# Two-bank PSUM tiles for the AV of batch 0: one normalisation and one x evacuation for two blocks

## The chip, the cores and the metric

The kernel runs on one core of a Trainium2 chip. The metric is the device time of one execution in microseconds (us). Several executions are made of each kernel; one more view, the profile, records every instruction of one of them. Engines: PE is TensorE, DVE is VectorE, ACT is ScalarE, POOL is GpSimd, SP is SyncE, which here only issues loads and stores.

## The reference

Eight batches of attention against pooled keys and values, and a two-layer MLP over all tokens.

```python
# q, k, v: (8, 8, 576, 64); w_in: (512, 2048); w_out: (2048, 512)
k_p = k.reshape(B, H, 72, 8, D).mean(axis=3)          # pool 8 keys to one
v_p = v.reshape(B, H, 72, 8, D).mean(axis=3)
scores = np.matmul(q, k_p.transpose(0, 1, 3, 2)) / np.sqrt(D)
attn = softmax(scores)
x = np.matmul(attn, v_p)                              # (B, H, S, D) -> (B*S, 512)
h = x @ w_in
out = (h - np.tanh(h)) @ w_out                        # (4608, 512) float32
```

## The kernel before

The kernel does the attention of batch 0 first, then the MLP of 512 tokens at a time, with the attention of the next batch woven between the MLP's matmuls. "AV" is the product of the exponentials with the pooled values. A column of ones beside V gives the sum of the exponentials, so a normalisation is a reciprocal of 4 columns and a multiplication. A "turn" is a transpose done on PE; the "q tail" is the load of the q rows of a batch's last 64 tokens; `warm_pe` runs idle matmuls, whose results nobody reads, where PE would wait.

```python
def av_half(b, blk, half, x_sb, alloc):               # one block of 128 tokens, 4 heads
    ps = alloc([128, 4, D1], FP32, "x_ps")            # one PSUM bank
    for n in range(3):
        ... # three matmuls into ps
    rden = work.tile([128, 4, 1], FP32, name="rden", tag="rden", bufs=4)
    nc.vector.reciprocal(out=rden[:, :, :], in_=ps[:, :, D:D1])
    nc.vector.tensor_tensor(out=x_sb[:, half, :, :], in0=ps[:, :, 0:D],
        in1=rden[:, :, :].to_broadcast([128, 4, D]), op=ALU.mult)

def x_pe_transpose(b, blk, x_sb, fbs=(0, 4)):         # turn x on PE, copy it to xT on ACT
    ps = ps_any([128, f1 - f0, 128], FP32, "xT_ps")
    ...
    nc.scalar.copy(out=xT[:, f0:f1, pos : pos + 128 - p0], in_=ps[:, :, p0:128])
...
after(load_k(1), w1_dmas[1])                          # batch 1's keys: after a weight load
load_q(1, False)
load_main(v_pairs, v_raw[1], 1, 0, NM)
...
load_left(v_pairs, v_raw[1], 1, nc.scalar)            # loads that ACT issues, ahead of
load_q_tail(1, q_raws[1], nc.scalar)                  # its x copies
...
av_half(0, 2, 0, xs[2], ps_all)                       # AV, turns, and the first
x_pe_transpose(0, 0, xs[0], (0, 2))                   # halves of five MLP tiles,
...                                                   # woven by hand
mlp_h_mms(0, 4, 0, 2, (ps_o, "o_ps"))
nc.scalar.copy(out=q_bf[:QT, R, :, :], in_=t0[:QT, :, R, :])
for i in range(5):
    mlp_h_mms(0, i, 2, 4)                             # their second halves
    mlp_h_act(i, gts)
...
pool_k(1, nc.gpsimd, mid=(2, 3))                      # batch 1's keys, pooled on POOL;
...                                                   # two w2 loads issued in the middle
for u in range(16):                                   # MLP output of the first 512 tokens
    mlp_o(0, tb, qd * 4, qd * 4 + 4, gts, o_pools[tb])
    if u == 2:
        k_transpose(1, ps_any, (nc.vector.tensor_copy, nc.vector.tensor_copy))
    if u == 3:
        q_pe_transpose(1, (0, 1), "act")
    ...
```

The softmax here doesn't subtract the row's maximum and nothing guards it: scores larger than these inputs give would overflow.

## Time and profile before

| | |
|---|---|
| time, median of 3 | 300.64 us (300.51 to 300.65) |
| span in the profile | 299.1 us |
| PE busy | 97% |
| granted PE clock | 1.00 |
| AV stretch of batch 0 | 14.6 to 21.3 us |
| PE reaches the key transposes of batch 1 | 37.3 us |
| they start | 37.82 us |

This is the timeline of PE (start, length, engine, line, operation, output and inputs, and in brackets how long the engine was idle and for whom):

```profile
18.49 0.59 PE L428 MATMUL hT_ps<-xT,w1b 128*128 128x512 bf16 x2 [0.28 <-ACT xT L397]
...
37.82 0.45 PE L259 MATMUL kT_ps<-ident,kd 128*128 128x128 bf16 x5 [0.52 <-POOL kd L206]
```

The first is the end of the AV stretch: the first MLP matmul waits for ACT's copies of x. The second is the wait for the keys.

### The profile page before, as it was taken

To read this page: it belongs to the slowest core of one execution; us is meant where nothing else is said; L and a number is where in the kernel's file an instruction comes from. 1 tells how busy PE (TensorE), PEld (TensorE's weight loads), DVE (VectorE), ACT (ScalarE), POOL (GpSimd) and SP (SyncE) were. 2 spreads that over 40 slices of the span, in tenths; PEclk is the share of its full clock that TensorE was granted. 3 is DMA by queue.
4 is the path that set the end of the run, shared out by engine and by line. 5 is a ranking of instruction groups with operands and counts; after the bars stand their busy time and mean duration, and the time that the engine had idled before them with its cause. 6 is when DMAs were issued, how large, how long until landed. Compare 5 with 4: busy or idle time off the path is not lost.

```text
span 299.1 us, 4694 instructions
## 1 busy us (share of the span) xinstructions
PE 291.5 (97%) x1671; PEld 142.5 (48%) x1671; DVE 159.1 (53%) x343; ACT 149.4 (50%) x283; POOL 115.5 (39%) x110
## 2 busy tenths in 40 slices
PE   7989999999999999999999999999999999999994
PEld 3454455544544454445444554455445544444443
DVE  5658665673547444753476247716680758108600
ACT  4647583666146633654265516650665166126511
POOL 8500904871496109922971089307940000000000
PEclk9999999999999999999999999999999999999999
DMA  7999999849854998699648974897431430111032
GB/s 251 226 211 278 311 227 310 263 87 328 234 113 99 271 297 134 117 302 245 107 88 235 300 167 94 242 294 159 97 66 35 95 92 0 37 70 36 0 72 70
DMA packets 66183, 49.79 MB, mean 166 GB/s; under 512 B 39920, under 2 KB 52976, under 8 KB 66160
## 3 DMA queue, kind: packets, MB, share of 16 engines
q1 hardware_dynamic: 58832, 42.94, 56.0%
q0 software_dynamic: 4752, 4.72, 9.4%
q10 hardware_dynamic: 2576, 1.84, 2.3%
q8 instruction: 13, 0.21, 0.3%
q14 instruction: 10, 0.08, 0.1%
HBM read 36.70 MB, written 9.44 MB: 154 GB/s over the span
## 4 chain that ended last, share of the span: by engine, by line
PE 85%; DMA 9%; POOL 4%; issue 0%; SPq 0%; ACT 0%; DVE 0%; POOLq 0%
PE o_ps L456 40%; PE hT_ps L428 37%; DMA w1b<-in_moe_w_in_dram 4%; PE x_ps L346 4%; DMA k_raw<-in_k_dram 4%; PE s_ps L298 3%; POOL k_raw L198 1%; DMA out_dram<-o_sb 1%; POOL k_raw L203 1%; POOL kd L206 1%; POOL w2b L510 0%; PE xT_ps L390 0%; POOL v_raw L576 0%; PE qT_ps L171 0%; POOL w1b L503 0%
## 5 line engine op out<-in xcount | busy, mean ns | idle before, releaser
L456 PE MATMUL o_ps<-w2b,gT 128*128 128x512 bf16 x560 | 134.4, 380 | 0.0
L441 DVE TENSOR_TENSOR gT<-hT_ps,t_sb 128x512 bf16<-128x512 f32 x144 | 98.9, 691 | 57.7 <-ACT t_sb L439 57.6
L428 PE MATMUL hT_ps<-xT,w1b 128*128 128x512 bf16 x576 | 126.9, 379 | 0.3 <-ACT xT L397 0.3
L439 ACT ACTIVATE t_sb<-hT_ps 128x512 f32<-128x512 f32 x144 | 85.6, 597 | 38.3 <-PE hT_ps L428 37.5
L428 PEld LDWEIGHTS <-w1b 128*128 128x128 bf16 x576 | 55.9, 98 | 66.5 <-issue 0.4
L456 PEld LDWEIGHTS <-gT 128*128 128x128 bf16 x560 | 52.5, 98 | 52.0 <-issue 1.4
L465 ACT COPY o_sb<-o_ps 128x512 f32<-128x512 f32 x33 | 19.3, 585 | 75.2 <-PE o_ps L456 75.2
L359 DVE RECIPROCAL rden<-x_ps 128x4 f32<-128x4 f32 x80 | 14.2, 177 | 52.5 <-PE x_ps L346 52.0
L360 DVE TENSOR_TENSOR x_sb<-x_ps,rden 128x256 bf16<-128x256 f32 x80 | 34.0, 425 | 3.5 <-DMA xT<-x_sb 0.6
L148 POOL CAST q_bf<-q_raw 128x2048 bf16<-128x2048 f32 x6 | 11.3, 1888 | 59.9 <-issue 34.8
L198 POOL TENSOR_TENSOR k_raw<-k_raw 128x1280 f32<-128x1280 f32 x7 | 20.2, 2886 | 27.4 <-DMA k_raw<-in_k_dram 16.6
L317 ACT ACTIVATE E<-s_ps 128x288 bf16<-128x288 f32 x60 | 21.4, 410 | 13.2 <-PE s_ps L298 13.0
L346 PE MATMUL x_ps<-VB,E 128*128 128x130 bf16 x240 | 20.8, 221 | 0.4 <-ACT xT L397 0.3
L346 PEld LDWEIGHTS <-E 128*128 128x128 bf16 x240 | 16.9, 98 | 8.8 <-DVE VB L230 0.6
L216 POOL TENSOR_TENSOR v_raw<-v_raw 128x1280 f32<-128x1280 f32 x6 | 17.4, 2898 | 0.0
L298 PE MATMUL s_ps<-qT,KB 128*128 128x288 bf16 (+5 forms) x128 | 17.0, 290 | 0.2
L298 PEld LDWEIGHTS <-KB 128*128 128x128 bf16 (+1 forms) x128 | 7.0, 96 | 10.2 <-issue 3.5
L527 PE MATMUL warm_ps<-xT 128*128 128x512 bf16 x29 | 10.2, 465 | 1.3 <-DVE xT L539 1.3
L206 POOL TENSOR_TENSOR kd<-k_raw 128x640 bf16<-128x640 f32 x7 | 10.8, 1540 | 0.5
L203 POOL TENSOR_TENSOR k_raw<-k_raw 128x640 f32<-128x640 f32 x7 | 10.8, 1541 | 0.5
L397 ACT CAST xT<-xT_ps 128x256 bf16<-128x256 f32 (+1 forms) x14 | 5.8, 436 | 8.5 <-PE xT_ps L390 5.1
L219 POOL TENSOR_TENSOR v_raw<-v_raw 128x640 f32<-128x640 f32 x6 | 9.3, 1544 | 0.5
(73 smaller groups left out, 100.7 us busy)
## 6 DMA issues: line engine op xcount, KB each, us to landing
k_raw<-in_k_dram SPq DMA_DIRECT2D x7, 1024.0 KB, 5.9
q_raw<-in_q_dram SPq DMA_DIRECT2D x7, 1024.0 KB, 10.2
v_raw<-in_v_dram SPq DMA_DIRECT2D x7, 1024.0 KB, 9.3
out_dram<-o_sb SPq DMA_DIRECT2D x38, 128.0 KB, 2.4
out_dram<-o_sb SPq DMA_DIRECT2D x16, 256.0 KB, 3.7
w1b<-in_moe_w_in_dram POOLq DMA_DIRECT2D x4, 512.0 KB, 14.2
w2b<-in_moe_w_out_dram POOLq DMA_DIRECT2D x4, 512.0 KB, 16.9
k_raw<-in_k_dram SPq DMA_DIRECT2D x7, 128.0 KB, 5.8
```

The costliest lines, as they stand in the source:

```text
L198: first = eng.tensor_tensor(out=r[:, :, 0:4, :], in0=r[:, :, 0:4, :], in1=r[:, :, 4:8, :], op=ALU.add)
L216: eng.tensor_tensor(out=r[:, :, 0:4, :], in0=r[:, :, 0:4, :], in1=r[:, :, 4:8, :], op=ALU.add)
L298: nc.tensor.matmul(dst[p : p + w], lhsT=KB[b % 2][:, o : o + w], rhs=qTs[b][:, m, c0:c1], start=True, stop=True,)
L317: nc.scalar.activation(out=E[:, t, half * hs : (half + 1) * hs], in_=ps[:, :], func=ACT.Exp, scale=SCALE)
L346: nc.tensor.matmul(ps[:, 2 * n : 2 * n + 2, :].rearrange("p h d -> p (h d)") if n < 2 else ps.rearrange("p (a s) d -> p a s d", s=2)[:, :, ...
L359: nc.vector.reciprocal(out=rden[:, :, :], in_=ps[:, :, D:D1])
L360: nc.vector.tensor_tensor(out=x_sb[:, half, :, :], in0=ps[:, :, 0:D], in1=rden[:, :, :].to_broadcast([128, 4, D]), op=ALU.mult,)
L428: nc.tensor.matmul(h_tiles[i][:, :], lhsT=w1b[:, fb, i * 128 : (i + 1) * 128], rhs=xT[:, fb, tok0 : tok0 + TG], start=(fb == 0), stop=(fb ...
L439: nc.scalar.activation(out=t_sb[:, :], in_=h_ps[:, :], func=ACT.Tanh)
L441: nc.vector.tensor_sub(out=gT[:, :], in0=h_ps[:, :], in1=t_sb[:, :])
L456: nc.tensor.matmul(o_ps[:, :], lhsT=gts[i][:, tb * 128 : (tb + 1) * 128], rhs=w2b[:, i, :], start=(i == 0), stop=(i == NHID - 1),)
L465: (nc.vector.tensor_copy if g == 0 and tb % 2 else nc.scalar.copy)(out=o_sb[:, :], in_=o_ps[:, :])
```

## The change

The intent is to halve the number of DVE and ACT instructions in the AV stretch of batch 0, for which PE waits there (0.39 us for DVE, 0.29 and 0.28 for ACT in the profile before). In the same profile, twice the elements take less than twice the time: a DVE multiplication out of PSUM 425 ns for 128x256 and 691 ns for 128x512, an ACT copy of x 375 and 590 ns. PSUM becomes one tile of eight banks with banks assigned by hand. A pair of blocks takes two neighbouring banks, so that one reciprocal, one multiplication and one copy serve both. Order and queues of all loads stay. The order of PE's work changes too, and the sequence has one idle matmul more (6 instead of 5).

```diff
+    psum = ctx.enter_context(tc.tile_pool(name="psum", bufs=1, space=PSUM))
+    PS = psum.tile([128, 8, 512], FP32, name="PS")
...  (ps_h, ps_o and ps_a become rotations over banks 0-2, 3-4 and 5-7)
+    def av_pair(p, half, b0):
+        ps = PS[:, b0 : b0 + 2, 0 : 4 * D1].rearrange("p k (h d) -> p k h d", d=D1)
+        for k in range(2):
+            av_mms(0, 2 * p + k, half, ps[:, k, :, :])
+        rden = work.tile([128, 2, 4, 1], FP32, name="rden2", tag="rden2")
+        nc.vector.reciprocal(out=rden[:, :, :, :], in_=ps[:, :, :, D:D1])
+        nc.vector.tensor_tensor(out=x0[:, 2 * p : 2 * p + 2, half, :, :],
+            in0=ps[:, :, :, 0:D], in1=rden[:, :, :, :].to_broadcast([128, 2, 4, D]), op=ALU.mult)
+    def x0_turn(blks, half, b0, eng):
+        ...  # turns of one or two blocks into one bank
+        eng(out=xT[:, 2 * half : 2 * half + 2, c : c + n * 128], in_=ps.rearrange("p f i c -> p f (i c)"))
+    av_pair(0, 0, 2)
+    av_pair(1, 0, 5)
+    av_pair(0, 1, 0)
+    warm_pe(1)
+    x0_turn((0, 1), 0, 7, nc.scalar.copy)
+    av_pair(1, 1, 2)
+    warm_pe(1)
+    x0_turn((2, 3), 0, 5, nc.scalar.copy)
+    warm_pe(2)
+    h_open(3, 4)
+    x0_turn((0, 1), 1, 7, nc.scalar.copy)
...  (h_open(0), h_open(1), last turns, h_open(2), h_open(4); the av_half sequence of before goes)
```

More of the change, by code (lines that the diff above doesn't have):

```diff
@@ L57, with bank, __init__, tile @@
     opool = ctx.enter_context(tc.tile_pool(name="opool", bufs=4))
-    ps_h = ctx.enter_context(tc.tile_pool(name="ps_h", bufs=3, space=PSUM))
-    ps_o = ctx.enter_context(tc.tile_pool(name="ps_o", bufs=2, space=PSUM))
-    ps_a = ctx.enter_context(tc.tile_pool(name="ps_a", bufs=3, space=PSUM))
+    psum = ctx.enter_context(tc.tile_pool(name="psum", bufs=1, space=PSUM))
+    PS = psum.tile([128, 8, 512], FP32, name="PS")
+    def bank(i, shape):
+        n = 1
+        for d in shape[1:]:
+            n *= d
+        v = PS[:, i, 0:n]
+        if len(shape) == 3:
+            return v.rearrange("p (a b) -> p a b", a=shape[1])
+        if len(shape) == 4:
+            return v.rearrange("p (a b c) -> p a b c", a=shape[1], b=shape[2])
+        return v
+    class Banks:
+        def __init__(self, *ids):
+            self.ids, self.n = ids, 0
+        def tile(self, shape, dtype=None, name=None, tag=None):
+            self.n += 1
+            return bank(self.ids[(self.n - 1) % len(self.ids)], shape)
+    ps_h = Banks(0, 1, 2)
+    ps_o = Banks(3, 4)
+    ps_a = Banks(5, 6, 7)
     ctx.enter_context(tc.manual_schedule())
@@ L81 @@
     warm = const.tile([128, 1], FP32, name="warm")
+    x0 = const.tile([128, 4, 2, 4, D], BF16, name="x0")
     VB = [const.tile([128, 3 * NM, D1], BF16, name=f"VB{i}") for i in range(2)]
@@ L336, in scores_tail, with av_mms @@
         )
-    def av_half(b, blk, half, x_sb, alloc):
+    def av_mms(b, blk, half, ps):
         E = E_tiles[b]
@@ L341, in av_half @@
         c0 = blk * 128 if blk < 4 else S - 128
-        ps = alloc([128, 4, D1], FP32, "x_ps")
         for n in range(3):
@@ L357, in av_half @@
             )
+    def av_half(b, blk, half, x_sb, alloc):
+        ps = alloc([128, 4, D1], FP32, "x_ps")
+        av_mms(b, blk, half, ps)
         rden = work.tile([128, 4, 1], FP32, name="rden", tag="rden", bufs=4)
@@ L424, in mlp_h_mms @@
         if f0 == 0:
-            p, tag = pool or (ps_h, "hT_ps")
-            h_tiles[i] = p.tile([128, TG], FP32, name="hT_ps", tag=tag)
+            h_tiles[i] = ps_h.tile([128, TG]) if pool is None else pool
         for fb in range(f0, f1):
@@ L521, in after, with warm_pe @@
             )
-    warm_ps = ps_o.tile([128, 512], FP32, name="warm_ps", tag="o_ps")
-    def warm_pe(n, cols=512):
+    def warm_pe(n, cols=512, b0=4):
         for _ in range(n):
             nc.tensor.matmul(
-                warm_ps[:, 0:cols], lhsT=zeros[:, 0:128], rhs=zeros[:, 0:cols], start=True, stop=True
+                bank(b0, [128, cols]), lhsT=zeros[:, 0:128], rhs=zeros[:, 0:cols], start=True, stop=True
             )
@@ L613, in q_turn, with v_pe_pool @@
         )
-    def v_pe_pool(t0, t1, turn):
-        ps = ps_any([128, t1 - t0, 1, D], FP32, "v_ps")
+    def v_pe_pool(t0, t1, turn, b0=None):
+        shape = [128, t1 - t0, 1, D]
+        ps = ps_any(shape, FP32, "v_ps") if b0 is None else bank(b0, shape)
         for j in range(POOL):
@@ L628, in ps_b1 @@
         return ps_a.tile(shape, dtype, name=name, tag="ps_a")
-    ps_all = ps_any
     q_turn(nc.scalar.copy, 0, 2)
@@ L655 @@
     v_left(VB[0], v_ps[:, 0, :, :], nc.vector)
-    vs = v_pe_pool(0, NM, ident)
+    vs = v_pe_pool(0, NM, ident, 4)
     v_main(VB[0], vs, nc.vector, 0, 2)
@@ L660 @@
     load_q_tail(1, q_raws[1], nc.scalar)
-    xs = [new_x() for _ in range(4)]
     gts = []
-    ps_o2 = lambda sh, dt, name: ps_o.tile(sh, dt, name=name, tag="o_ps")
-    ps_h2 = lambda sh, dt, name: ps_h.tile(sh, dt, name=name, tag="hT_ps")
-    warm_pe(2)
-    av_half(0, 0, 0, xs[0], ps_all)
-    av_half(0, 1, 0, xs[1], ps_all)
-    av_half(0, 2, 0, xs[2], ps_all)
-    x_pe_transpose(0, 0, xs[0], (0, 2))
-    av_half(0, 3, 0, xs[3], ps_all)
-    warm_pe(1)
-    x_pe_transpose(0, 1, xs[1], (0, 2))
@@ L673 @@
-    ps_any = ps_b1
-    av_half(0, 0, 1, xs[0], ps_h2)
-    warm_pe(1)
-    x_pe_transpose(0, 2, xs[2], (0, 2))
-    av_half(0, 1, 1, xs[1], ps_b1)
-    warm_pe(1)
-    x_pe_transpose(0, 3, xs[3], (0, 2))
-    av_half(0, 2, 1, xs[2], ps_o2)
-    mlp_h_mms(0, 0, 0, 2)
-    x_pe_transpose(0, 0, xs[0], (2, 4))
-    av_half(0, 3, 1, xs[3], ps_b1)
-    mlp_h_mms(0, 1, 0, 2)
-    x_pe_transpose(0, 1, xs[1], (2, 4))
-    mlp_h_mms(0, 2, 0, 2)
-    x_pe_transpose(0, 2, xs[2], (2, 4))
-    x_pe_transpose(0, 3, xs[3], (2, 4))
@@ L689 @@
-    mlp_h_mms(0, 3, 0, 2, (ps_o, "o_ps"))
-    mlp_h_mms(0, 4, 0, 2, (ps_o, "o_ps"))
+    def av_pair(p, half, b0):
[4 more added lines that the diff above has]
+        nc.vector.reciprocal(out=rden[:, :, :, :], in_=ps[:, :, :, D:D1])
+        nc.vector.tensor_tensor(
+            out=x0[:, 2 * p : 2 * p + 2, half, :, :],
+            in0=ps[:, :, :, 0:D],
+            in1=rden[:, :, :, :].to_broadcast([128, 2, 4, D]),
+            op=ALU.mult,
+        )
@@ new lines, in x0_turn @@
+    def x0_turn(blks, half, b0, eng):
+        n = len(blks)
+        ps = bank(b0, [128, 2, n, 128])
+        for i, blk in enumerate(blks):
+            for f in range(2):
+                nc.tensor.matmul(
+                    ps[:, f, i, :],
+                    lhsT=x0[:, blk, half, 2 * f : 2 * f + 2, :].rearrange("p h d -> p (h d)"),
+                    rhs=ident[:, :],
+                    start=True,
+                    stop=True,
+                )
+        c = blks[0] * 128
+        eng(
+            out=xT[:, 2 * half : 2 * half + 2, c : c + n * 128],
+            in_=ps.rearrange("p f i c -> p f (i c)"),
+        )
@@ new lines, in h_open @@
+    def h_open(i, b0):
+        mlp_h_mms(0, i, 0, 2, bank(b0, [128, TG]))
+    warm_pe(2, b0=3)
+    av_pair(0, 0, 2)
[6 more added lines that the diff above has]
+    x0_turn((2, 3), 0, 5, nc.scalar.copy)
+    warm_pe(2)
+    h_open(3, 4)
+    x0_turn((0, 1), 1, 7, nc.scalar.copy)
+    h_open(0, 0)
+    h_open(1, 1)
+    x0_turn((2,), 1, 5, nc.scalar.copy)
+    x0_turn((3,), 1, 6, nc.vector.tensor_copy)
@@ L691 @@
+    h_open(2, 2)
+    h_open(4, 3)
+    ps_any = ps_b1
+    ps_h.n = ps_o.n = 0
     nc.scalar.copy(out=q_bf[:QT, R, :, :], in_=t0[:QT, :, R, :])
```

## The prediction

The forecast's sum is 0.55 us saved in the AV stretch and 0.55 us more waited at the key transposes, zero at the end. Passages that told of the hardware what no trace of this case shows are cut from the text below and marked. None of them was a term of this sum.

> **What bounds the kernel now.** I read the page first. TensorE (PE) is busy for 97% of the span at the full granted clock; no other engine passes 53%.
>
> ```profile
> span 299.1 us, 4694 instructions
> PE 291.5 (97%) x1671; PEld 142.5 (48%) x1671; DVE 159.1 (53%) x343; ACT 149.4 (50%) x283; POOL 115.5 (39%) x110
> PEclk9999999999999999999999999999999999999999
> ```
>
> So only stretches in which PE waits can give time back. I cut the span into stretches (the table of windows: length, then busy time of PE, weight loads, DVE, ACT, POOL). The AV work of batch 0, which is all the change touches, lies in the first row.
>
> ```profile
> 14.60:21.30 6.70, 5.72 (x54) 3.59 (x55) 4.59 (x17) 2.85 (x9) 0.00 (x0) 1.00 1.23 212
> 21.30:37.30 16.00, 15.68 (x89) 7.22 (x87) 11.67 (x21) 10.91 (x20) 7.00 (x5) 1.00 1.14 288
> 37.90:60.00 22.10, 22.10 (x167) 12.10 (x168) 14.40 (x34) 13.43 (x25) 10.01 (x6) 1.00 0.99 264
> 60.00:295.00 235.00, 235.00 (x1293) 113.85 (x1291) 119.25 (x244) 112.92 (x216) 87.30 (x73) 1.00 0.59 145
> ```
>
> PE has about 1 us of idle time in the AV stretch. From 37.9 us to the end it has none. Between the two there is one more wait, in the list of who waited for whom (PE, first 60 us: total, times, longest):
>
> ```profile
> PE xT_ps L390 <- DVE x_sb L360: 0.7, 2, 0.4
> PE kT_ps L259 <- POOL kd L206: 0.5, 1, 0.5
> PE x_ps L346 <- ACT xT L397: 0.3, 1, 0.3
> PE hT_ps L428 <- ACT xT L397: 0.3, 1, 0.3
> ```
>
> The second line decides. At 37.3 us PE has reached the transposes of batch 1's keys and waits for GpSimd (POOL) to finish pooling them. The chain of work that ended last, in order of time (start, length, what), says where that wait comes from:
>
> ```profile
> 5.86 12.86 DMA w1b<-in_moe_w_in_dram
> ...
> 19.21 10.84 DMA k_raw<-in_k_dram
> ...
> 30.21 2.90 POOL k_raw L198
> 33.11 1.47 POOL w2b L510 x2
> ...
> 34.58 1.58 POOL k_raw L203
> ...
> 36.23 1.55 POOL kd L206
> ...
> 37.82 0.45 PE kT_ps L259 x5
> 38.27 0.86 PE o_ps L456 x4
> ```
>
> The reader is to see that this chain **goes around the AV stretch**: a weight load that lands at 18.7 us releases batch 1's key load, it lands at 30.05, POOL needs 30.2 to 37.8 for it, and only then PE takes over and never stops again. Nothing in it is AV, x, or the first MLP tiles. AV lies on a second branch that arrives at 37.3, with 0.52 us to spare.
>
> [...] a DVE TENSOR_TENSOR out of PSUM takes 425 ns for 256 elements and 691 for 512, so 266 ns per 256 elements and about 159 ns fixed. [...] each of two blocks' groups has its own bank, and only the DVE reads run across two. No trace of before has such a read. [...] Before has waits up to 1.3 us and stays at clock 1.00; I expect none above 1.3 us after.
>
> **The change part by part.** The instruction order of both kernels shows the PE stream before and after the AV part unchanged, POOL and SP with the same waits in the same order, and ACT's loads still ahead of its first x copy.
>
> *Removed on DVE:* 8 reciprocals and 8 multiplications become 4 and 4. The timeline of before shows the pace:
>
> ```profile
> 15.00 0.18 DVE L359 RECIPROCAL rden<-x_ps 128x4 f32<-128x4 f32 x1
> 15.22 0.42 DVE L360 TENSOR_TENSOR x_sb<-x_ps,rden 128x256 bf16<-128x256 f32 x1
> 15.56 0.17 DVE L359 RECIPROCAL rden<-x_ps 128x4 f32<-128x4 f32 x1
> ```
>
> One half-block costs 0.55 us start to start (reciprocal to reciprocal), eight 4.4 us. A pair adds 256 elements, 0.27 us, so 0.82 us; four are 3.3 us. DVE saves 1.1 us. *Removed on ACT:* eight copies of 128x256 (0.37 us) become three of 128x512 (some 0.59 us), one of 128x256, and one 128x256 copy on DVE. *Unchanged on PE:* 24 AV matmuls, 16 turns, 4 warming matmuls and 10 first-half MLP matmuls in the stretch; only their order moves.
>
> *The stretch walked through (estimates from the trace).* PE starts AV at 14.6 as before. Six matmuls instead of three before the first reciprocal: 15.17 instead of 15.00. DVE multiplications end at about 16.06, 16.88, 17.70 and 18.52 (before: the eighth at 20.06). PE turns blocks 0 and 1 at 16.1, blocks 2 and 3 at 16.95. ACT cannot copy before about 16.95 in either kernel, since a load issue holds it:
>
> ```profile
> 16.28 0.62 ACTq L127 DMA_DIRECT2D q_raw<-in_q_dram  x1
> 16.95 0.92 ACT L397 CAST xT<-xT_ps 128x256 bf16<-128x256 f32 x3 [3.19 <-PE x_ps L346]
> ```
>
> Two copies of 128x512 end at about 18.05, and the first MLP matmul starts at 18.1 (before: 18.49). From there PE has 10 of these (0.215 us each) and 8 turns (0.055 us each) to do, 2.6 us, with x ready in time: the second halves of the MLP tiles start at about 20.7. Before they started at 20.41 + 4 x 0.215 = 21.27. So the stretch gives PE **0.55 us** (0.3 to 0.9, as the walk rests on several handovers).
>
> *What comes of it.* PE then reaches the key transposes at 37.30 - 0.55 = 36.75. POOL still ends at 37.78. PE starts them at 37.82 as before, and its wait grows from 0.52 to about 1.07 us. Sum: 0.55 saved, 0.55 waited, **zero** at the end.
>
> **The rivals.** *A, the gain comes through:* the end moves by the 0.55 us, to 300.1. It would need the key load to be early by as much. [...] Against it: the releases (a weight load at 18.7), competitors and issue order are the same, and the three runs of before lie within 0.14 us. *B, the new order is slower:* two blocks in one tile make the first turn wait longer, and shared-bank reads get extra waits between DVE and ACT in the instruction order. To cost anything, PE must arrive over 0.52 us later than before; I find the added waits on work already finished. A loss of 1 us would give 301.1. *C, the key chain itself moves:* x0 and the single PSUM tile change addresses[...]. Each tenth would show in full, in either direction; POOL's first pooling step is 2.90 us both for batch 1 and for batch 2, beside different DVE work, so I give this a few tenths at most. *D, a clock drop through a longer PE gap:* a wait of 1.1 us is below the 1.3 us that did no harm at the start.
>
> **Range and chances.** Zero transfer gives 300.6, my prediction. Rival A, whole or partly, reaches to 300.1; C or a mild B to 301.0. To be 2% off it would take 6 us, while the whole AV stretch is 6.7 us long and has 1 us of idle: 1% on each side.
>
> **What would show it.** Right: DVE's reciprocals in the stretch number 4, 0.8 us apart; the MLP's second halves start near 20.7; the key load still lands near 30.05 and POOL ends near 37.8; PE's wait for it is near 1.1 us; from there both timelines agree to the end. Wrong: a PE wait of 0.5 us or less there with an earlier start of the key transposes (A or C), a wait of none at all (B), or new PE idle time after 38 us, which would mean that the new bank order costs something in the steady part.

## The result, and the profile after

The changed kernel took 300.72 us (median of 4, 300.60 to 300.74), the kernel before beside it 300.64 us (median of 4, with one run at 301.79). The ratio is 0.9993, with a 95% interval of 0.9969 to 1.0018: the same. Ratios are the mean time of one kernel's fast runs over that of the other's of the same rounds, so not quite the ratio of the medians.

The page and the table of stretches of the changed kernel (length, then busy time of PE, weight loads, DVE, ACT, POOL):

```profile
span 299.0 us, 4704 instructions
...
14.60:21.30 6.70, 6.03 (x56) 3.75 (x56) 4.01 (x10) 2.54 (x5) 0.00 (x0) 1.00 1.24 212
21.30:37.30 16.00, 15.37 (x88) 7.01 (x85) 11.67 (x21) 10.85 (x20) 7.15 (x5) 1.00 1.14 289
37.90:60.00 22.10, 22.10 (x167) 12.08 (x165) 14.39 (x34) 13.25 (x25) 10.18 (x6) 1.00 0.98 263
```

PE does 0.31 us more work in the AV stretch (6.03 against 5.72) and 0.31 us less in the next one (15.37 against 15.68). (The busy time of the first stretch includes the added idle matmul; that PE is 0.31 us ahead shows in the block 4 turn below, which comes at 32.44 instead of 32.75 us.) What was gained in the first stretch was waited for in the second. The list of who waited for whom (PE, first 60 us) names the wait, and the chain of work that ended last is the old one:

```profile
PE PS L282 <- POOL kd L229: 0.7, 1, 0.7
PE PS L453 <- ACT xT L712: 0.6, 1, 0.6
```

```profile
5.87 12.56 DMA w1b<-in_moe_w_in_dram
18.93 10.97 DMA k_raw<-in_k_dram
30.06 2.90 POOL k_raw L221
...
36.09 1.55 POOL kd L229
37.69 0.45 PE PS L282 x5
```

L282 are the key transposes, L229 the last pooling step. The DVE and ACT timelines in the AV stretch:

```profile
15.14 0.21 DVE L691 RECIPROCAL rden<-PS 128x8 f32<-128x8 f32 x1 [0.27 <-PE PS L368]
15.38 0.69 DVE L692 TENSOR_TENSOR x<-PS,rden 128x512 bf16<-128x512 f32 x1
...
15.99 0.20 DVE L691 RECIPROCAL rden<-PS 128x8 f32<-128x8 f32 x1
...
16.56 0.62 ACTq L150 DMA_DIRECT2D q_raw<-in_q_dram  x1
...
17.23 1.07 ACT L712 CAST xT<-PS 128x512 bf16<-128x512 f32 x2 [3.48 <-PE PS L368]
...
18.35 0.59 PE L453 MATMUL PS<-xT,w1b 128*128 128x512 bf16 x2 [0.55 <-ACT xT L712]
```

A pair takes 0.84 us on DVE. But ACT, held by its load issue until batch 0's q tail has landed (at 16.54 us here, 16.26 in the profile before; the last section says how this was read), starts copying at 17.23 us, 0.28 us later than in the profile before, so the first MLP matmul comes at 18.35, only 0.14 us earlier than before.

**An account of the start.** Call M the moment when PE turns block 4 of batch 0, the only other PE wait between 21 us and the keys (0.32 us for DVE, alike in both kernels). All profiles with the key transposes in their old place fit one rule: they start at the later of M + 4.38 us (PE's own work) and 0.06 us after POOL has finished, and the end comes 261.3 us after them.

| profile | M | keys pooled | key transposes start | end minus that |
|---|---|---|---|---|
| before | 32.75 | 37.76 | 37.82 | 261.3 |
| after | 32.44 | 37.63 | 37.69 | 261.3 |
| e9 (below) | 32.86 | 38.26 | 38.32 | 261.3 |
| e10 (below) | 33.78 | 37.37 | 38.16 | 261.3 |

The 4.38 is measured in e10, where PE did not wait. It also shows that the idle time printed before the transposes is about 0.17 us short, since it counts from a modelled end of the last matmul: the slack of PE before was 37.82 - 37.13 = 0.69 us, and after 37.69 - 36.82 = 0.87 us.

### The profile page after: what moved, and what is told of

Same layout as the page of the kernel before. It is cut to its first block, busy times and chain, and to the rows that moved or that the text cites. A ratio compares the mean times of both kernels' runs of the same rounds, so it can differ in the third digit from the quotient of the medians.

```text
span 299.0 us, 4704 instructions
## 1 busy us (share of the span) xinstructions
PE 291.5 (97%) x1672; PEld 142.8 (48%) x1672; DVE 158.4 (53%) x336; ACT 148.8 (50%) x279; POOL 115.7 (39%) x110
## 4 chain that ended last, share of the span: by engine, by line
PE 85%; DMA 9%; POOL 4%; issue 0%; SPq 0%; ACT 0%; DVE 0%; POOLq 0%; DVEq 0%
PE PS L481 40%; PE PS L453 37%; DMA w1b<-in_moe_w_in_dram 4%; PE PS L368 4%; DMA k_raw<-in_k_dram 4%; PE PS L321 3%; POOL k_raw L221 1%; DMA out_dram<-o_sb 1%; POOL k_raw L226 1%; POOL kd L229 1%; POOL w2b L535 0%; PE PS L416 0%; POOL v_raw L599 0%; PE PS L194 0%; POOL w1b L528 0%
## 5 line engine op out<-in xcount | busy, mean ns | idle before, releaser
L481 PE MATMUL PS<-w2b,gT 128*128 128x512 bf16 x560 | 134.3, 379 | 0.0
L466 DVE TENSOR_TENSOR gT<-PS,t_sb 128x512 bf16<-128x512 f32 x144 | 98.9, 691 | 56.9 <-ACT t_sb L464 56.7
L453 PE MATMUL PS<-xT,w1b 128*128 128x512 bf16 x576 | 126.8, 379 | 0.6 <-ACT xT L712 0.6
L464 ACT ACTIVATE t_sb<-PS 128x512 f32<-128x512 f32 x144 | 85.6, 597 | 38.5 <-PE PS L453 37.7
L490 ACT COPY o_sb<-PS 128x512 f32<-128x512 f32 x33 | 19.3, 586 | 75.2 <-PE PS L481 75.2
L385 DVE RECIPROCAL rden<-PS 128x4 f32<-128x4 f32 x72 | 12.8, 177 | 52.6 <-PE PS L368 52.3
L171 POOL CAST q_bf<-q_raw 128x2048 bf16<-128x2048 f32 x6 | 11.3, 1890 | 60.2 <-issue 34.2
L386 DVE TENSOR_TENSOR x_sb<-PS,rden 128x256 bf16<-128x256 f32 x72 | 30.6, 424 | 2.9 <-DMA xT<-x_sb 0.4
L340 ACT ACTIVATE E<-PS 128x288 bf16<-128x288 f32 x60 | 21.4, 409 | 13.2 <-PE PS L321 13.0
L368 PE MATMUL PS<-VB,E 128*128 128x130 bf16 x240 | 20.2, 220 | 0.1
L321 PE MATMUL PS<-qT,KB 128*128 128x288 bf16 (+5 forms) x128 | 17.0, 289 | 0.2
L229 POOL TENSOR_TENSOR kd<-k_raw 128x640 bf16<-128x640 f32 x7 | 10.8, 1539 | 0.5
```

The lines of the kernel that those rows point to most:

```text
L321: nc.tensor.matmul(dst[p : p + w], lhsT=KB[b % 2][:, o : o + w], rhs=qTs[b][:, m, c0:c1], start=True, stop=True,)
L340: nc.scalar.activation(out=E[:, t, half * hs : (half + 1) * hs], in_=ps[:, :], func=ACT.Exp, scale=SCALE)
L368: nc.tensor.matmul(ps[:, 2 * n : 2 * n + 2, :].rearrange("p h d -> p (h d)") if n < 2 else ps.rearrange("p (a s) d -> p a s d", s=2)[:, :, ...
L453: nc.tensor.matmul(h_tiles[i][:, :], lhsT=w1b[:, fb, i * 128 : (i + 1) * 128], rhs=xT[:, fb, tok0 : tok0 + TG], start=(fb == 0), stop=(fb ...
L464: nc.scalar.activation(out=t_sb[:, :], in_=h_ps[:, :], func=ACT.Tanh)
L466: nc.vector.tensor_sub(out=gT[:, :], in0=h_ps[:, :], in1=t_sb[:, :])
```

## The experiments

My theory: batch 1's key chain (weight load, key load, pooling on POOL) sets the end, so the AV saving becomes waiting time. The rivals: the AV saving is not real, or it would be lost at another place anyway. All runs below gave correct results. Those of one group ran on the same chip beside the same runs of the kernel before.

### First group: the key transposes one step later

```diff
-        if u == 2:
+        if u == 3:
             k_transpose(1, ps_any, (nc.vector.tensor_copy, nc.vector.tensor_copy))
-        if u == 3:
             q_pe_transpose(1, (0, 1), "act")
```

On the kernel before:

> The kernel before, with the key transposes of batch 1 taken one MLP-output step later on PE (0.86 us later). Theory (the chain of weight load, key load and POOL pooling decides when PE may go on, AV does not): the 0.5 us wait before the key transposes vanishes, PE has no idle there, and the time falls by about 0.5 us, to 300.1. Rival (the end is set by a later load or by work after the transposes): the wait comes back at another place and the time stays within 0.15 us of 300.64.

On the changed kernel:

> The changed kernel with the same shift of the key transposes. Theory: its wait there (0.7 us in the profile) vanishes, so the time falls by about 0.7 us against the changed kernel, to about 300.0 or a little lower, and it is now faster than the shifted kernel before by what the AV stretch saved, 0.3 us as measured where PE arrives. Rival (the AV saving is not real, or is lost elsewhere): equal to the shifted kernel before within 0.1 us.

Measured: 300.93 us (300.76 to 301.27) and 300.86 us (300.66 to 301.08), ratios to the kernel before 0.9998 and 0.9993, interval about 0.002 to each side. Neither fell; both expectations missed. The PE timeline of the shifted kernel before shows that I had built a new wait:

```profile
39.16 0.40 PE L171 MATMUL qT_ps<-ident,q_bf 128*128 128x128 bf16 x4 [0.74 <-DVE KB L250]
```

The three transposes now follow each other without MLP work between, in three rotating banks, and the fourth waits until DVE has emptied the first. The key wait was exchanged for a bank wait of 0.74 us. In the changed kernel POOL also finished at 37.97 us, so 0.52 us of the key wait remained besides. The edit was wrong for its purpose and decides nothing.

The same shift with ACT's last load issue moved behind the x copies:

```diff
-    load_q_tail(1, q_raws[1], nc.scalar)
 ...
+    load_q_tail(1, q_raws[1], nc.scalar)
     nc.scalar.copy(out=q_bf[:QT, R, :, :], in_=t0[:QT, :, R, :])
```

> As the previous one, and ACT issues the load of batch 1's q tail after the x copies instead of before them. Theory (ACT, held by this issue until 16.9 to 17.2 us, sets when the first MLP matmul may start, so it took half of the predicted 0.55 us): the first x copy starts near 16.35, the first MLP matmul near 18.05 instead of 18.35, and the time falls by another 0.2 to 0.3 us. Rival (the DVE normalisations set it): the MLP start moves by less than 0.1 us and the time stays.

Measured: 317.02 us (311.01 to 318.76). The ACT and PE timelines show what went wrong:

```profile
28.56 0.63 ACTq L150 DMA_DIRECT2D q_raw<-in_q_dram  x1
...
31.11 5.28 PE L453 MATMUL PS<-xT,w1b 128*128 128x512 bf16 x12 [7.87 <-DVE gT L466]
```

In the new order the load has another completion counter, that of batch 1's key load, and its issue waits until that load has landed, at 28.54 us (the profile gives the idle time of ACT that ends there, 8.70 us, to `DMA k_raw<-in_k_dram`). The issue is made only at 28.56 us and holds all of ACT's tanh work behind it. PE stood for 7.87 us, and its granted clock fell from 1.00 (20 to 22 us) to the 0.77 and 0.67 below (the last three figures of a row of the table of stretches are the granted clock, the DMA share and GB/s):

```profile
22.00:31.00 9.00, 1.25 (x6) 0.49 (x5) 0.63 (x2) 1.77 (x4) 1.52 (x1) 0.77 1.15 274
31.00:40.00 9.00, 8.88 (x37) 3.68 (x38) 6.24 (x11) 4.81 (x10) 5.95 (x5) 0.67 1.14 291
```

This attempt says nothing about the change.

The last of the group undid the merged normalisation:

```diff
-        nc.vector.reciprocal(out=rden[:, :, :, :], in_=ps[:, :, :, D:D1])
-        nc.vector.tensor_tensor(out=x0[:, 2 * p : 2 * p + 2, half, :, :], ...)
+        for k in range(2):
+            nc.vector.reciprocal(out=rden[:, k, :, :], in_=ps[:, k, :, D:D1])
+            nc.vector.tensor_tensor(out=x0[:, 2 * p + k, half, :, :], ...)
```

> As the shifted changed kernel, but each block has its own reciprocal and multiplication again (8 and 8 instead of 4 and 4), from the same two-bank tiles. Theory by the durations of before: a pair takes 1.1 us on DVE instead of 0.84, so the last normalisation ends some 1.0 us later, near 19.6; PE then waits for the last turns (at 19.65 with the merged form) by a few tenths, and the time is 0.1 to 0.4 us longer than with merged normalisation. Rival (merging the normalisation is worth nothing, ACT alone decides): the same time within 0.1 us.

Measured: 300.92 us (300.50 to 301.24), against 300.86 with merged normalisation: the same. With the bank wait in both, the time cannot tell; the profile is used below.

### Second group: the key wait taken away

The three edits, the same on both kernels:

```diff
-    pool_k(1, nc.gpsimd, mid=(2, 3))
+    pool_k(1, nc.gpsimd, mid=(2,))
+    load_w2(3)
 ...
-        if u == 2:
-            k_transpose(...)
         if u == 3:
-            q_pe_transpose(1, (0, 1), "act")
+            k_transpose(...)
+            q_pe_transpose(1, (0,), "act")
         if u == 4:
-            q_pe_transpose(1, (2,), "act")
+            q_pe_transpose(1, (1, 2), "act")
```

On the kernel before:

> The kernel before with the key wait taken away without touching AV, and without the bank wait that the first shift brought (0.74 us at the second q transpose): POOL issues one of the two w2 loads after pooling the keys instead of between its steps (some 0.75 us less in the key chain), the key transposes come one MLP-output step later, and the q transposes are spread over the next two steps. Theory: no PE wait between 33 and 60 us, and the end is 0.5 us earlier than before, 300.1 to 300.2. Rival (something else sets the end): a new wait, and the time stays near 300.7.

On the changed kernel:

> The changed kernel with the same three edits. Theory (AV saves 0.3 to 0.65 us on PE and only the key wait swallowed it): no PE wait there and 0.3 to 0.65 us less than the kernel before with these edits, 299.5 to 299.9. Rival (the AV saving is lost elsewhere too): equal to the kernel before with these edits within 0.1 us.

Measured: the kernel before with these edits 300.30 us (300.26 to 300.47), ratio to the kernel before 0.9982 (0.9970 to 0.9995), which is some 0.55 us less (0.15 to 0.9 by the interval). The changed kernel with them 300.01 us (299.99 to 300.20), ratio 0.9974 (0.9961 to 0.9986), 0.8 us less. The runs of the two do not overlap, and their means differ by 300.33 - 300.07 = 0.26 us. The lists of waits show no PE wait for batch 1's keys in either. Their key transposes in the timelines carry no idle time; first the kernel before with the edits, then the changed one:

```profile
38.19 0.44 PE L259 MATMUL kT_ps<-ident,kd 128*128 128x128 bf16 x5
```

```profile
37.87 0.44 PE L282 MATMUL PS<-ident,kd 128*128 128x128 bf16 x5
```

The timeline of the second from 34 to 60 us has only this one gap left, at the MLP's output. The row has three matmuls where its neighbours have four, so a record may be missing there rather than PE idle:

```profile
45.39 0.81 PE L481 MATMUL PS<-w2b,gT 128*128 128x512 bf16 x3 [0.16 <-issue]
```

So the theory holds, both ways round: the same AV change that moved nothing in the tuned kernel is worth 0.26 us once the key chain is out of the way, and the key chain alone was worth some 0.55 us to the kernel before. This is just below the 0.3 to 0.65 us that I expected. The two profiled executions, one of each kernel, suggest why: AV started at 14.68 us in the kernel before with the edits and at 15.08 in the changed one, where PE had waited 0.6 us for batch 0's own keys instead of 0.3. From the AV start to the key transposes the changed kernel took 0.72 us less (ACT was held by its load issue in the first and not in the second), and the later start took back 0.40. With the key wait gone nothing hides the scatter of the start any more, so it is in every time of the freed kernels; whether the later start is chance was not tested.

The third moved the q tail load to SP, behind the q load, so that it holds nobody:

```diff
+    t1 = q_raws[1]
     load_q(1, False)
+    load_q_tail(1, t1, nc.sync)
     load_main(v_pairs, v_raw[1], 1, 0, NM)
 ...
-    load_q_tail(1, q_raws[1], nc.scalar)
```

> As the previous one, with batch 1's q tail load issued by SP behind the q load, so that ACT is not held before its first x copy, and the load doesn't end up behind the key load's completion counter as it did in the failed attempt. Theory: first x copy near 16.35 instead of 16.9 to 17.2, first MLP matmul near 18.0, wait of PE for x below 0.25 us, and 0.1 to 0.4 us less than the previous kernel. Rival (DVE sets it): the same time within 0.1 us.

Measured: 300.35 us (300.15 to 300.40), ratio 0.9981: 0.22 us slower than without it, by the means. The first x copy came at 16.40 and the first MLP matmul at 17.88 us, near what was expected. But AV had started early in this execution (14.43 against 15.08 us), and counted from there the first copy came 1.97 us later with and without the edit: ACT was not held in the profile of e6 either, so this pair does not measure the hold. PE then ran into the load of q, which landed no earlier:

```profile
37.88 0.40 PE L194 MATMUL PS<-ident,q_bf 128*128 128x128 bf16 x4 [0.23 <-ACT q_bf L171]
...
39.83 0.38 PE L321 MATMUL PS<-qT,KB 128*128 128x512 bf16 x1 [0.23 <-ACT qT L119]
```

L171 is the cast of batch 1's q, which began at 36.78 us when q had landed (36.63 in the previous kernel). The end came 261.2 us after the key transposes, against 260.4 in the previous kernel. Behind the keys, q is the next chain that PE may not overtake.

The fourth undid the merged normalisation in the freed kernel (the edit is shown above):

> The changed kernel freed of the key wait (as two above), but each block normalised by itself again (8 reciprocals and 8 multiplications). With nothing downstream to hide it, merging is worth what this run loses: by the durations some 1.0 us of DVE time, of which PE sees 0.1 to 0.6 us, as the last turns then wait for DVE. Rival (merging is hidden, only the copies count): within 0.1 us of the freed changed kernel.

Measured: 300.16 us (299.89 to 300.25), against 300.01 merged; the means are 300.13 and 300.07. The difference of 0.05 us is within the scatter (about 0.18 us to each side, by the spread of the two sets of five runs): no gain from merging the normalisations is shown, as the rival said, but one of 0.1 or 0.2 us is not excluded.

### Third group: PE time added to the AV stretch

Idle matmuls into a free bank, in the changed kernel as it was (2, then 5 of 0.215 us):

```diff
+    warm_pe(2, b0=7)
     for i in range(5):
         mlp_h_mms(0, i, 2, 4)
```

> The changed kernel as it was, with 2 idle matmuls of 128x512 (0.43 us of PE time) put in at the end of the AV stretch. Theory (PE arrives at the key transposes with 0.5 to 1 us to spare and only waits there): PE arrives 0.43 us later, the key wait shrinks by as much, from about 0.7 to about 0.3 us, and the time stays within 0.1 us of the changed kernel's 300.7. Rival (PE time in the AV stretch goes straight to the end): plus 0.43 us.

> The same with 5 idle matmuls (1.08 us). Theory: the first 0.7 us or so disappear in the key wait, which goes to zero, and only the rest, 0.3 to 0.5 us, reaches the end. Rival: plus 1.08 us.

Measured: 300.98 us (300.82 to 301.34) and 301.20 us (300.87 to 301.54); the kernel before beside them 300.64 us. Five matmuls cost 0.48 us against the changed kernel's 300.72 of the first measurement, where 1.08 us had been added, as expected, and they took the key wait to zero. By the account above, though, 1.08 us less the slack of 0.87 leaves only 0.21; in the profile ACT's first copy also came 0.35 us later after the AV start than in the changed kernel's, so the size of 0.48 is partly luck. Two cost 0.26 us instead of under 0.1. The profile of the run with two shows that the wait had not shrunk:

```profile
38.32 0.45 PE L282 MATMUL PS<-ident,kd 128*128 128x128 bf16 x5 [0.91 <-POOL kd L229]
```

PE came 0.42 us later, as it should, but the keys were pooled at 38.26 us, 0.63 us later than in the changed kernel's profile, because the weight load landed later (at 19.13 against 18.43 us). The profiled end moved by about what the keys moved (0.61 us), not by the dose. The idle matmuls ran from 20.94 us, after that landing, so they can't have delayed it. The times of this pair alone don't prove the slack. The account above, in which all four profiles fit, does not depend on it.

The freed changed kernel with both merges undone (normalisation as above, and the copies):

```diff
-        eng(out=xT[..., c : c + n * 128], in_=ps.rearrange("p f i c -> p f (i c)"))
+        for i, blk in enumerate(blks):
+            eng(out=xT[..., c + i * 128 : c + (i + 1) * 128], in_=ps[:, :, i, :])
```

> The changed kernel freed of the key wait, with both merges undone: each block has its own normalisation and its own copies, so the instruction sizes are those of before, and only the new order and the new bank plan of the changed kernel remain. If the merges are what saves, this falls back to the freed kernel before (0.25 us slower than the freed changed kernel). If the order and the banks save (no PE wait for a bank that ACT still reads), it loses 0.1 us or less. By the durations: copies in pairs of 0.37 us overlap to 0.65 against 0.59 us, so 0.1 us for the two that stand ahead of the MLP; I expect 0.1 to 0.2 us in all.

Measured: 300.23 us, but from 299.83 to 301.27, so the time is inconclusive. In the profile PE lost 1.4 us before AV, waiting for batch 0's own keys, which landed late in that execution.

The last was an attempt at the fastest version: the freed kernel with the tail on SP, and q transposes, scores and AV of batch 1 one step later.

```diff
-            q_pe_transpose(1, (0,), "act")        # u == 3
+            q_pe_transpose(1, (0, 1, 2), "act")   # u == 4, with scores at 5 to 9, AV at 10 to 14
```

> An attempt at the fastest version: the freed changed kernel with the q tail issued by SP, in which PE then waited 0.2 us for the q cast and 0.2 us for the q copies; here the q transposes, the scores and the AV of batch 1 come one MLP-output step later, past the landing of q. Theory (each wait met so far is a load chain of batch 1): both waits vanish and the time is 0.3 to 0.5 us below that kernel, 299.8 to 300.0 or a little lower. Rival (the later AV brings a new wait in the next stage): no gain.

Measured: 300.96 us (300.40 to 302.34): no gain. Its profile lost 2.3 us to batch 0's late keys, and the later AV brought a new wait of 0.56 us before the MLP of the second group of tokens, as the rival said. **The fastest version that I measured is the freed changed kernel (e6), 300.01 us against 300.83 us for the kernel before in the same rounds, 0.26% less.**

### What the profiles say of the AV stretch itself

In every profile but that of the failed e3 I took the time from the first AV matmul to M, less the idle matmuls that were added, and the time from the first AV matmul to ACT's first x copy.

| profile | first x copy | AV start to M | difference |
|---|---|---|---|
| before / e1 / e5 | 2.34 / 2.19 / 2.45 | 18.14 / 18.00 / 18.26 | 15.80 / 15.81 / 15.81 |
| after / e2 / e9 / e10 | 2.63 / 2.44 / 2.55 / 2.98 | 17.84 / 17.66 / 17.76 / 18.19 | 15.21 / 15.22 / 15.21 / 15.21 |
| e8, normalisation split | 2.61 | 17.82 | 15.21 |
| e4, normalisation split | 2.42 | 17.77 | 15.35 |
| e6 / e7 / e12, copy not held | 1.97 / 1.97 / 1.97 | 17.54 / 17.53 / 17.54 | - |
| e11, both split, copy not held | 1.94 | 17.82 | - |

While ACT is held by its load issue, the stretch ends a constant time after ACT's first copy: 15.81 us in the kernel before and 15.21 in the changed one. So **the change saves 0.60 us at the same start of ACT**. In the first pair of profiles ACT started 0.29 us later after the change, which hid half of that; whether that was chance was not tested. With normalisations split, the saving is still 0.60 us when the hold is long (e8) and 0.46 us when it is shorter (e4). With ACT free the merged form ends at 17.54, and with both merges undone at 17.82, 0.28 us later (e11, one profile). No profile of the kernel before has ACT free, so how the 0.60 us divide between the merges and the new order of PE and banks stays open.

## Why the prediction was right or wrong

**The end does not move.** Right, and shown: the chain around AV is the same after the change, the key wait took what PE gained (stretches of the profile), and with the key wait removed from both kernels the gain appears (e5 and e6).

**The AV stretch gives 0.55 us (0.3 to 0.9).** The first pair of profiles gave 0.31 us, the same ACT start gives 0.60. The mechanism was right; the term of the walk that was mis-sized in that pair is "ACT cannot copy before about 16.95 in either kernel": it was 17.23, since the load issue came at 16.56 instead of 16.28 us, after a q tail that landed at 16.54 instead of 16.26. The first MLP matmul came at 18.35, not 18.1, and this carried through.

**DVE saves 1.1 us.** The DVE pace of a pair was 0.84 us, not 0.82; the four normalisations did end at 18.6 us, not 20.06. But that saving was mostly not what PE waited for: undoing it left the stretch as long as it was when ACT was held long (e8) and made it 0.14 us longer when the hold was shorter (e4). In the prediction I let the whole walk seem to rest on it, while the walk itself ended at ACT's copies. The prediction also counts 4 warming matmuls as unchanged; the kernels have 5 before and 6 after. The added one runs just before a PE wait of 0.55 us for ACT, so it cost nothing there.

**The wait grows from 0.52 to about 1.07 us.** The profile shows 0.69. Of the difference, 0.24 us is the smaller AV gain and 0.14 us is that the keys were pooled earlier in that execution (37.63 against 37.76 us). Both waits, 0.52 and 0.69, are printed 0.17 us too small, as the account shows.

**The rivals.** A, the gain comes through, was wrong for the tuned kernel. B, extra waits between DVE and ACT: none was seen, and PE had no wait after 38 us. C, the chain itself moves: it did, by 0.14 us, and the span went from 299.1 to 299.0 us. Its scatter is larger than I said from three runs: in the seven profiles with an unchanged key chain and an undisturbed PE, POOL finished between 37.37 and 38.26 us, and the kernel before ranged from 300.39 to 302.75 us over all groups. My "a few tenths at most" was too small. D, a lower clock: no, it was 0.999 to 1.000 in the changed kernel's runs. The failed attempt with 7.87 us of PE idle time had 0.971 to 0.989, and the longest run of the kernel before (302.75 us) had 0.991.

## What to carry to other kernels

Before pricing a saving, follow the chain that ended last and look for a branch that joins it later: a stage with idle time on the busiest engine is worth nothing while the next stage begins with a wait on something that does not depend on it. To find out what a change is worth in itself, take away the wait that hides it from both kernels, and check that the edit did not make a new one; here rotating banks (a wait of 0.74 us), a shared completion counter (7.87 us) and the next load (0.23 us) did so in three attempts. When two profiles differ by tenths of a microsecond, compare a stage from its own start and from the event that releases it, not in absolute time.

## What the traces show of the hardware

- A DVE multiplication out of PSUM took 425 ns for 128x256 and 691 ns for 128x512 in the profile before.
- A DVE read across two banks cost nothing extra in the profile after: 691 ns for 128x512 over two banks, 691 ns for 128x512 in one.
- The landing of the same load moved between executions. The MLP weight load at the head of the key chain landed at 18.43 us in the profile of the changed kernel and at 19.13 in that with two added matmuls, 0.70 us later; the keys were then pooled 0.63 us later and the end came 0.61 us later.
- A load's issue held the compute instructions behind it on the same engine for as long as an earlier load kept the completion counter that it was to use. In the tuned order the traces of both kernels give the load the same semaphore as batch 0's q tail, and its issue waits for that semaphore. The last update of the semaphore before that issue, the landing of that tail, came at 16.26 us before and 16.54 us after the change, and the issue at 16.28 and 16.56. In the wrong order tried here the issue waited for batch 1's key load, which landed at 28.54 us, and held ACT until 28.56.
- In the failed e3, with 7.87 us of PE idle time, the granted clock was 0.77 in the mean from 22 to 31 us, 0.67 from 31 to 40 and 0.98 from 40 to 62, while PE had resumed at 31.11; waits of up to 1.3 us left it at 1.00 in the profiles before and after.
